# Gated linear attention with a feed-forward network: blocks of two chunks of two batches, and a gather in two steps

## The chip, the cores and the metric

The kernel runs on one core of a Trainium2 chip. The metric is the device time of one execution in microseconds, the median of several runs.

## The reference

Four batches (B), eight heads (H), 768 tokens (S), 48 values in a head (D). A state of 48 by 48 per batch and head is scaled row by row with alpha, gets the outer product of k and v added, and is read with q. The outputs of the heads, side by side, are rows of 384 for 3072 tokens; they go through a feed-forward network (FFN) of 2048 hidden values with a leaky ReLU. The two weights come as 64-bit floats.

```python
for t in range(S):
    state = alpha[:, :, t, :, None] * state + np.einsum('bhd,bhe->bhde', k[:, :, t], v[:, :, t])
    y[:, :, t] = np.einsum('bhd,bhde->bhe', q[:, :, t], state)
...
h = x @ w_in
g = np.maximum(0.01 * h, h)
return (g @ w_out).astype(np.float32)
```

## The kernel before, in words

**Units and blocks.** The attention works on *units*: one chunk of 128 tokens of one batch, with all eight heads. There are 6 chunks and 4 batches, so 24 units, u0 to u23. Four units are a *block* of 512 tokens, and the FFN works on blocks, 0 to 5. Before, a block is one chunk of all four batches, so that the unit which needs a batch's state comes four units behind the one that made it.

**A unit's steps**, in the order of `attention`: `scans` (alpha transposed, its running products pc and rc, on DVE), `scores` (k times q on PE, L348; its wait for the finished ks is what the profile calls L339), `mask_scores` (the triangle: either an ACT copy, L358, and a select on POOL, L359, or one multiplication on DVE, L356; `on_pe` units take two copies and selects, the others one of each kind), `k_tokens` (L371), the next unit's `scaled_q` and `scaled_k`, and `outputs`: the state times q (L388) and the masked scores times v (L394) give y, k times v gives the state's addition kv (L405), then y is split into a high part xh (ACT, L411) and a rest xl (DVE, L412). `next_state` adds to the state (L424 on ACT for the first chunk, L426 on DVE) and POOL scales it (L364). Units u0 to u7, u10 and u11 are transposed on PE (L272), the others on DVE (L281).

**x and the gather.** x lies in the tile `large`, whose 128 partitions are 2 x (48 + 16) rows. Three slots hold six heads in 48 of each 64 rows; heads 6 and 7 are written to a fourth, shared staging slot, and once the four units of a block are there, `gather` moves their rows by two DMAs on SP's queue (L435, 192 KB each) into the 16 free rows of the other three slots. There are seven slots: three for even blocks, three for odd, one staging slot for both. A block's first xh writes the staging slot, so it comes behind the gather of the block before.

**The FFN.** For each of 16 slices of the hidden values, `ffn_in` makes nine matmuls of 512 columns (L479, into `ph`: high and low parts of x and weight), ACT and DVE make the leaky ReLU (L482, L485) and split it into gh and gl (L487, L490), and `ffn_out` makes nine matmuls (L509). Blocks 0 to 4 are written transposed: DVE transposes the result (L526), and SP stores it in pieces of 32 columns of one batch (L531, 16 KB; 16 stores for one of three groups, 48 for a block). Block 5 is written straight.

**The order of the work.** First the attention of blocks 0 and 1 runs, with the first two weight slices converted from 64 bits beside it and the first `ph` groups of block 0 (`STARTS`). Then the FFN of blocks 0 and 1 runs together while the other slices are converted. From block 2 on a block's FFN runs alone, with the steps of later units strewn in by a count (`SL`, `LEAD`, `HELD`). `behind(key)` orders an instruction after another one in the scheduling and adds no semaphore. A scheduler with its own timeline then sets each engine's order; each engine works through its instructions in that order, and SP issues nearly all DMAs in its own.

## Time and profile before

| | |
|---|---|
| runs shown | 566.86, 567.15 and 569.07 us |
| median | 567.15 us |
| the profiled execution | 569.6 us |
| its span in the trace | 567.9 us |
| instructions | 9071 |
| DMA engines, mean share | 39.5% (hardware queue) |

The span runs from the first to the last instruction of the trace. PE is TensorE, PEld its weight loads, DVE VectorE, ACT ScalarE, POOL GpSimd, SP SyncE; SPq is SP's queue. A row of a timeline gives the start and the length in us, the engine, the line, the operation, the tile written and the tiles read, the size, and xN for N instructions alike in a row; in brackets stands how long the engine was idle before it and what ended that. A row of windows gives the stretch, its length, the busy time of PE, PEld, DVE, ACT and POOL, the granted TensorE clock (1.00 is full speed), the DMA share and GB/s. A matmul of plain f32 counts as two in the trace (x8 in the program is x16 there). In the 40 slices a digit is the busy share in tenths, a slice is 14.2 us.

### The profile page before, as it was taken

The numbers are of one execution on the slowest core, as the hardware profiler recorded it, in microseconds if no ns is written. First come the engines' busy times: TensorE is split into PE (matmuls) and PEld (weight loads), VectorE is DVE, ScalarE is ACT, GpSimd is POOL, SyncE is SP. The second block draws the span as 40 slices with busy tenths as digits, with TensorE's granted clock in tenths as the row PEclk, the third lists the DMA queues.
The fourth block names the chain that finished last, engine by engine and source line by source line (L and its number), as shares of the span: only waits on it lengthen the run. The fifth ranks groups of instructions, "written<-read, shape, count | busy, mean of one in ns | idle before, by whom it ended". The sixth has DMA issues, their size and how long they took to land.

```text
span 567.9 us, 9071 instructions
## 1 busy us (share of the span) xinstructions
PE 525.9 (93%) x3262; PEld 439.5 (77%) x3262; DVE 382.9 (67%) x644; ACT 217.5 (38%) x409; POOL 65.0 (11%) x140
## 2 busy tenths in 40 slices
PE   8986869999999999289899999999999999999995
PEld 7765658888887778178788888888888888888994
DVE  6886669889889869519987788577766343343331
ACT  2654534445453334223334334324332432232321
POOL 4444400000000013210211100100100000000000
PEclk9996879999999999659999999999999999999998
DMA  9999333244374122775644633441312101011001
GB/s 148 179 180 194 110 83 99 70 110 113 91 177 72 37 34 44 138 169 108 140 87 102 113 92 58 84 98 27 68 23 34 15 1 29 1 29 28 1 0 61
DMA packets 125795, 46.09 MB, mean 81 GB/s; under 512 B 94960, under 2 KB 123120, under 8 KB 125744
## 3 DMA queue, kind: packets, MB, share of 16 engines
q1 hardware_dynamic: 125744, 45.45, 39.5%
q8 instruction: 27, 0.44, 0.4%
q14 instruction: 24, 0.20, 0.1%
HBM read 38.34 MB, written 4.72 MB: 76 GB/s over the span
## 4 chain that ended last, share of the span: by engine, by line
PE 81%; DVE 8%; DMA 4%; SPq 2%; issue 2%; ACT 1%; POOL 0%; DVEq 0%; ACTq 0%; POOLq 0%
PE ph L479 33%; PE a L509 25%; PE b L509 7%; PE b L394 4%; PE b L348 3%; PE b L388 3%; DMA large<-large 2%; PE b L272 1%; PE ph L165 1%; SPq L531 1%; DVE ks L281 1%; DVE rc L312 1%; PE b L405 1%; DMA small<-in_q_dram 1%; DVE pc L306 1%
## 5 line engine op out<-in xcount | busy, mean ns | idle before, releaser
L479 PE MATMUL ph<-large,w 128*128 128x512 f32 x864 | 219.8, 399 | 8.8 <-DMA large<-large 4.3
L479 PEld LDWEIGHTS ph<-large,w 128*128 128x128 f32 x864 | 162.7, 191 | 44.8 <-issue 5.2
L509 PE MATMUL a<-gh,w 128*128 128x512 f32 x384 | 130.3, 393 | 0.0
L485 DVE TENSOR_TENSOR t<-ph,t 128x512 f32<-128x512 f32 x96 | 65.4, 681 | 93.6 <-ACT t L482 93.5
L482 ACT ACTIVATE t<-ph 128x512 f32<-128x512 f32 x96 | 57.3, 597 | 143.0 <-PE ph L479 140.5
L487 ACT CAST gh<-t 128x512 fp32r<-128x512 f32 x96 | 59.6, 621 | 119.9 <-DVE t L485 117.1
L490 DVE TENSOR_TENSOR gl<-t,gh 128x512 fp32r<-128x512 f32 x96 | 65.8, 685 | 28.0 <-ACT gh L487 19.4
L509 PEld LDWEIGHTS a<-gh,w 128*128 128x128 f32 x384 | 72.0, 188 | 16.0 <-issue 0.6
L509 PE MATMUL a<-gl,w 128*128 128x512 f32 x192 | 75.0, 390 | 0.0
L348 PE MATMUL b<-qs,ks 48*128 48x128 f32 x320 | 31.8, 292 | 12.8 <-DVE ks L339 12.5
L509 PEld LDWEIGHTS a<-gl,w 128*128 128x128 f32 x192 | 36.1, 188 | 7.1
L348 PEld LDWEIGHTS b<-qs,ks 48*128 48x128 f32 x320 | 27.0, 194 | 18.2 <-issue 16.0
L359 POOL TENSOR_SCALAR_AFFINE_SELECT sm<-sm 128x512 f32<-128x512 f32 x34 | 26.0, 775 | 105.5 <-ACT sm L358 105.5
L509 PE MATMUL b<-gh,w 128*128 128x512 f32 x96 | 33.7, 404 | 0.0
L364 POOL TENSOR_TENSOR small<-us,pe 48x192 f32<-48x192 f32 x40 | 22.4, 559 | 76.0 <-DVE us L426 67.0
L316 POOL COPY pe<-pc 128x4 f32<-128x4 f32 x24 | 6.3, 261 | 207.3 <-DVE pc L306 207.1
L394 PE MATMUL b<-sm,small 128*48 128x128 f32 (+1 forms) x368 | 28.6, 279 | 0.2
L388 PE MATMUL b<-qs,small 112*112 112x128 f32 x152 | 21.9, 291 | 6.2 <-DVE large L412 5.8
L388 PEld LDWEIGHTS b<-qs,small 112*112 112x112 f32 x152 | 20.2, 190 | 8.4 <-issue 6.2
L358 ACT COPY sm<-b 128x512 f32<-128x512 f32 x26 | 15.2, 587 | 26.5 <-PE b L348 26.4
L509 PE MATMUL a<-w,gh 128*128 128x384 f32 x96 | 24.3, 338 | 0.0
L394 PEld LDWEIGHTS b<-sm,small 128*48 128x48 f32 (+1 forms) x368 | 20.9, 125 | 4.2 <-POOL sm L359 1.4
(96 smaller groups left out, 622.4 us busy)
## 6 DMA issues: line engine op xcount, KB each, us to landing
raw<-in_moe_w_out_dram SPq DMA_DIRECT2D x16, 384.0 KB, 3.5
small<-in_v_dram SPq DMA_DIRECT2D x24, 192.0 KB, 3.8
raw<-in_moe_w_in_dram SPq DMA_DIRECT2D x32, 144.0 KB, 4.0
out_dram<-o SPq DMA_DIRECT2D x240, 16.0 KB, 1.5
small<-in_alpha_dram SPq DMA_DIRECT2D x30, 96.0 KB, 2.3
small<-in_q_dram SPq DMA_DIRECT2D x28, 96.0 KB, 2.3
small<-in_k_dram SPq DMA_DIRECT2D x28, 96.0 KB, 2.4
large<-large SPq DMA_DIRECT2D x12, 192.0 KB, 4.7
```

Of the source, the lines that this page charges most:

```text
L348: nc.tensor.matmul(ss[s][:, p, :], ks[lo:lo + D, p, :], qs[lo:lo + D, p, :], start=True, stop=True)
L358: made["sm", u] = nc.scalar.copy(sm[s], ss[s])
L359: nc.gpsimd.affine_select(out=sm[s], in_=sm[s], compare_op=ALU.is_ge, fill=0.0, base=0, pattern=[[0, NP], [1, C]], channel_multiplier=-1)
L364: nc.gpsimd.tensor_tensor(*scalings.pop(0))
L388: nc.tensor.matmul(y[0:BR, (p + turn) % NP, :], W[0:BR, p, :], qs[0:BR, p, :], start=p == 0, stop=False, skip_group_check=True)
L394: nc.tensor.matmul(y[lo:lo + m, (p + turn) % NP, :], V[:, c:c + m], masked[u][s][:, p, :], start=not tb and p == 0, stop=p == NP - 1, skip ...
L479: nc.tensor.matmul(ph, w_in_of(f, wn, g), xt[:, g, :], start=n == 0, stop=n == 3 * NG - 1)
L482: put(ordered, "ACT", lambda: nc.scalar.mul(t, ph, 0.01))
L485: put(ordered, "DVE", lambda: nc.vector.tensor_tensor(t, ph, t, ALU.max))
L487: put(ordered, "ACT", lambda: nc.scalar.copy(gh, t))
L490: made["gl", i, f] = put(ordered, "DVE", lambda: nc.vector.tensor_tensor(gl, t, gh.bitcast(F32), ALU.subtract))
L509: nc.tensor.matmul(po, *((w[:, js], gt) if turned else (gt[:, js], w)), start=f == 0 and n == 0, stop=f == NF - 1 and n == 2,)
```

## The change

1. The units are put in another order: a block is now two chunks of two batches, u0 to u3 = (chunk 0, batch 0), (0, 1), (1, 0), (1, 1). `place` gives a unit's columns within x, so that a batch's two chunks stand side by side. A batch's state is now needed two units after it was made (or six). The first chunks' units are u0, u1, u4, u5, the last chunks' u18, u19, u22, u23.
2. x has eight slots: each parity of block has its own staging slot, and the `turn` of the heads is gone.
3. The gather goes in two steps: behind a block's third unit the columns 0 to 384 (four DMAs of 72 KB), behind the fourth the columns 384 to 512 (four of 24 KB). Block 2's are issued on ScalarE's queue, the others on SP's.
4. `mask_scores`: the second half goes to DVE for all units from u6 on; before, u6, u7, u10 and u11 had two ACT copies and two POOL selects.
5. The first output group of block 0 is ordered behind the last y of u7, and some later steps behind other keys ("w", "in", "gl").
6. The transposed output: a store now takes two chunks of one batch (32 KB), so there are 8 stores for a group and 24 for a block.

```diff
-    UPB = B
+    UPB = 4
-    units = [(t, b) for t in range(NC) for b in range(B)]
+    units = [(t0 + t, b0 + b) for t0 in range(0, NC, 2) for b0 in range(0, B, 2) for t in (0, 1) for b in (0, 1)]
...
+    def place(u):
+
+        tb, b = units[u]
+        j = b % 2 * 2 + tb % 2
+        return slice(j * C, (j + 1) * C)
...
-    x_sb, = pieces("large", F32R, (2 * NG + 1, 2, TB))
+    x_sb, = pieces("large", F32R, (2 * (NG + 1), 2, TB))
...
-            if s and not on_pe(u):
+            if s and u >= AHEAD - 2:
...
-        at = i % 2 * NG
-
-        turn = i % 2
+        at = i % 2 * (NG + 1)
...
-        xh, xl = (x_sb[0:BR, at:at + NP, n, j * C:(j + 1) * C] for n in (0, 1))
+        xh, xl = (x_sb[0:BR, at:at + NP, n, place(u)] for n in (0, 1))
...
-    def gather(i):
-
-        at, last = i % 2 * (NG + 1), NG
+    def gather(i, *cols):
+
+        at = i % 2 * (NG + 1)
         xs[i] = [x_sb[:, at:at + NG, n, :] for n in (0, 1)]
-        x = x_sb.bitcast(F32)
-        for lo in (0, HB):
-            made["g", i] = nc.sync.dma_start(
-                x[lo + D:lo + HB, at:at + NG].rearrange("r g n t -> r g (n t)"), x[lo:lo + D, last].rearrange("r n t -> r (n t)")
-            )
+        x = x_sb.bitcast(F32)[:, :, :, slice(*cols)]
+        queue = nc.scalar if i == 2 else nc.sync
+        for n in (0, 1):
+            for lo in (0, HB):
+                made["g", i] = queue.dma_start(x[lo + D:lo + HB, at:at + NG, n], x[lo:lo + D, at + NG, n])
...
-                if u % UPB == UPB - 1:
-                    gather(u // UPB)
+                if u % UPB == UPB - 2:
+                    gather(u // UPB, 0, TB - C)
+                elif u % UPB == UPB - 1:
+                    gather(u // UPB, TB - C, TB)
...
-                for b in range(B):
-                    r = b * S + i * C
+                for n, u in enumerate((i * UPB, i * UPB + 1)):
+                    tb, b = units[u]
+                    r = b * S + tb * C
...
-                        out[r:r + C, c:c + 32].rearrange("(m r) c -> r m c", r=32),
-                        t[32 * a:32 * (a + 1)].rearrange("r (b m c) -> r b m c", b=B, c=32)[:, b],
+                        out[r:r + 2 * C, c:c + 32].rearrange("(m r) c -> r m c", r=32),
+                        t[32 * a:32 * (a + 1)].rearrange("r (b m c) -> r b m c", b=2, c=32)[:, n],
...
-    put_out()
+    with behind("y", AHEAD - 1):
+        put_out()
...
-            with behind("gl", 0, f + FORE):
+            with behind("w", f + FORE + 1) if f + FORE + 1 < NF else behind("gl", 0, f + FORE):
...
-                    with (behind("gl", i, f - 1) if f else behind("x", (i + 1) * UPB - 1)) if held else nullcontext():
+                    with ExitStack() as holds:
+                        if held:
+                            holds.enter_context(behind("in", i, f))
+                            holds.enter_context(behind("gl", i, max(f - 1, 0)))
```

How instructions move shows in the engines' orders. PE at the end of block 1's attention, before: L388 and L394 are u7's y, L405 its kv, `ph` the first matmuls of a slice of block 0, L509 the first output group.

```order
153 L371 MATMUL b<-small,ks 128x112 x4
154 L388 MATMUL a<-qs,small 112x128 x4
155 L479 MATMUL ph<-large,w_786 128x512 x2
156 L394 MATMUL a<-sm,small 48x128
157 L405 MATMUL b<-small,ktok 48x48 x8
158 L509 MATMUL b<-gh,w_571 128x512
159 L509 MATMUL b<-gl,w_571 128x512
160 L509 MATMUL b<-gh,w_571 128x512 x2
161 L509 MATMUL b<-gl,w_571 128x512
162 L509 MATMUL b<-gh,w_571 128x512
163 L394 MATMUL a<-sm,small 48x128 x7
164 L509 MATMUL b<-gh,w_571 128x512
```

The same place after (eight lines further down in the code: L394 and L400 are y, L411 kv, L517 the output group):

```order
152 L379 MATMUL b<-small,ks 128x112 x4
153 L394 MATMUL a<-qs,small 112x128 x4
154 L487 MATMUL ph<-large,w_791 128x512 x2
155 L411 MATMUL b<-small,ktok 48x48 x8
156 L400 MATMUL a<-sm,small 48x128 x8
157 L517 MATMUL b<-gh,w_585 128x512
158 L517 MATMUL b<-gl,w_585 128x512
159 L517 MATMUL b<-gh,w_585 128x512 x2
160 L517 MATMUL b<-gl,w_585 128x512
```

The output group, which stood between y's first matmul and the other seven, now stands behind all eight, and kv ahead of them.

SP between the stores of blocks 0 and 1 and the gather of block 2, before: L531 are stores, L140 and L152 the loads of later units, L435 the gather.

```order
97 L133 DMA small<-in_alpha_dram 128x8x48
98 L531 DMA out_dram<-o 32x4x32 x32
99 L152 DMA small<-in_v_dram 128x8x48
100 L531 DMA out_dram<-o 32x4x32 x16
101 L140 DMA small<-in_alpha_dram 32x4x192 x2
102 L140 DMA small<-in_alpha_dram 32x4x160 x2
103 L140 DMA small<-in_q_dram 32x4x192 x2
104 L140 DMA small<-in_q_dram 32x4x160 x2
105 L140 DMA small<-in_k_dram 32x4x192 x2
106 L140 DMA small<-in_k_dram 32x4x160 x2
107 L152 DMA small<-in_v_dram 128x8x48
108 L435 DMA large<-large 16x3x1024 x2
```

After, L540 are the stores; no gather stands here, since block 2's is on ACT:

```order
103 L141 DMA small<-in_alpha_dram 128x8x48
104 L540 DMA out_dram<-o 32x8x32 x24
105 L160 DMA small<-in_v_dram 128x8x48
106 L148 DMA small<-in_alpha_dram 32x4x192 x2
107 L148 DMA small<-in_alpha_dram 32x4x160 x2
108 L148 DMA small<-in_q_dram 32x4x192 x2
109 L148 DMA small<-in_q_dram 32x4x160 x2
```

Between the same two loads stand 24 stores instead of 48.

PE at the start of block 2's FFN, before: L348 are the scores of u12, behind which stand its other matmuls and then the first three groups of block 2.

```order
455 L348 MATMUL b<-qs,ks 128x128 x8
456 L371 MATMUL b<-small,ks 128x112 x4
457 L388 MATMUL b<-qs,small 112x128 x4
458 L394 MATMUL b<-sm,small 48x128
459 L405 MATMUL b<-small,ktok 48x48 x8
460 L479 MATMUL ph<-large,w_571 128x512 x9
461 L479 MATMUL ph<-large,w_786 128x512 x9
462 L479 MATMUL ph<-large,w_897 128x512 x9
```

After, rows 445 to 449 are u11's matmuls, and block 2's groups follow at once (a group's first matmul stands apart in two of them):

```order
445 L356 MATMUL b<-qs,ks 128x128 x8
446 L379 MATMUL b<-small,ks 128x112 x4
447 L394 MATMUL b<-qs,small 112x128 x4
448 L400 MATMUL b<-sm,small 48x128 x8
449 L411 MATMUL b<-small,ktok 48x48 x8
450 L487 MATMUL ph<-large,w_585 128x512
451 L487 MATMUL ph<-large,w_791 128x512
452 L487 MATMUL ph<-large,w_585 128x512 x8
453 L487 MATMUL ph<-large,w_791 128x512 x8
454 L487 MATMUL ph<-large,w_907 128x512 x9
```

u12's scores come 25 rows further down, among block 2's output groups.

More of the change, by code (lines that the diff above doesn't have):

```diff
@@ L377, in outputs @@
         tb, b = units[u]
-        i, j = divmod(u, UPB)
+        i = u // UPB
         pe, qs, ktok = live[u][:3]
         V, W = vals_sb[u % NV], state[b]
-        at = i % 2 * NG
-        turn = i % 2
+        at = i % 2 * (NG + 1)
         y = banks4()
@@ L388, in outputs @@
                 nc.tensor.matmul(
-                    y[0:BR, (p + turn) % NP, :], W[0:BR, p, :], qs[0:BR, p, :], start=p == 0, stop=False, skip_group_check=True
+                    y[0:BR, p, :], W[0:BR, p, :], qs[0:BR, p, :], start=p == 0, stop=False, skip_group_check=True
                 )
@@ L393, in outputs @@
                 c = (2 * p + s) * D
-                nc.tensor.matmul(
-                    y[lo:lo + m, (p + turn) % NP, :], V[:, c:c + m], masked[u][s][:, p, :],
+                made["y", u] = nc.tensor.matmul(
+                    y[lo:lo + m, p, :], V[:, c:c + m], masked[u][s][:, p, :],
                     start=not tb and p == 0, stop=p == NP - 1, skip_group_check=True,
@@ L478, in ffn_in @@
             for wn, xt in ((HIGH, xh), (HIGH, xl), (LOW, xh)):
-                nc.tensor.matmul(ph, w_in_of(f, wn, g), xt[:, g, :], start=n == 0, stop=n == 3 * NG - 1)
+                made["in", i, f] = nc.tensor.matmul(ph, w_in_of(f, wn, g), xt[:, g, :], start=n == 0, stop=n == 3 * NG - 1)
                 n += 1
@@ L505, in ffn_out @@
         for j, po in enumerate(pos[i]):
-            js = slice(j * P, (j + 1) * P)
+            js = slice(j * P, (j + 1) * P) if turned else place(i * UPB + j)
             for n, (gt, wn) in enumerate(((gh, HIGH), (gl, HIGH), (gh, LOW)) if turned else ((gh, HIGH), (gh, LOW), (gl, HIGH))):
```

## The prediction

> **What bounds the kernel now.** I read the page first: its busy times and its slices show which engine is short and where it isn't full.
>
> ```profile
> span 567.9 us, 9071 instructions
> PE 525.9 (93%) x3262; PEld 439.5 (77%) x3262; DVE 382.9 (67%) x644; ACT 217.5 (38%) x409; POOL 65.0 (11%) x140
> ...
> PE   8986869999999999289899999999999999999995
> ...
> PEclk9996879999999999659999999999999999999998
> ```
>
> PE is busy for 93% of the span, and its matmuls are the same before and after the change. So a gain can only come from the slices in which PE waits or has a low clock. A slice is 14.2 us: the weak ones are the first six (0 to 85 us) and those at 227 to 256 us. I then read PE's timeline there, which names the end of each wait. First place, near 47 us (columns: start, us, engine, line, operation, count, and in brackets the idle time before it):
>
> ```profile
> 47.48 2.02 PE L388 MATMUL b<-qs,small 112*112 112x128 f32 x8 [5.81 <-DVE large L412]
> 49.29 1.06 PE L272 MATMUL b<-small 128*128 128x128 f32 x4
> 52.34 0.73 PE L479 MATMUL ph<-large,w 128*128 128x512 f32 x2
> ...
> 56.60 0.60 PE L272 MATMUL b<-small 128*128 128x128 f32 x4
> 57.03 1.04 PE L388 MATMUL b<-qs,small 112*112 112x128 f32 x8
> ```
>
> ```profile
> 46.02 0.58 ACT L411 CAST large<-b 112x512 fp32r<-112x512 f32 x1 [6.29 <-DMA large<-large]
> ```
>
> ```profile
> 39.88 6.04 DMA large<-large
> 71.92 4.68 DMA large<-large
> ```
>
> The last two rows are from the chain: both gathers lie on it. At 46.02 ACT copies the first xh of block 1 and has waited 6.29 us for block 0's gather, because both blocks stage heads 6 and 7 in one slot. PE waits behind it for 5.81 us and then runs at a low clock: the same eight matmuls take 2.02 us here and 1.04 at 57.03, the same four transposes 1.06 and 0.60.
>
> Second place, 62 to 82 us, the last unit of block 1 (u7):
>
> ```profile
> 62.30 3.28 POOL L359 TENSOR_SCALAR_AFFINE_SELECT sm<-sm 128x512 f32<-128x512 f32 x2 [0.68 <-ACT sm L358]
> ```
>
> ```profile
> 65.05 0.39 PE L394 MATMUL a<-sm,small 128*48 128x128 f32 x1 [2.62 <-POOL sm L359]
> ...
> 66.22 0.80 PE L509 MATMUL b<-gh,w 128*128 128x512 f32 x1
> ...
> 68.86 1.07 PE L394 MATMUL a<-sm,small 128*48 128x128 f32 x14
> ...
> 76.74 5.03 PE L479 MATMUL ph<-large,w 128*128 128x512 f32 x11 [4.27 <-DMA large<-large]
> ```
>
> PE waits 2.62 us for u7's masks. It has begun y when six matmuls of the first output group cut in at 66.22 (2.64 us to 68.86), then y ends, xh, xl and the gather follow, and PE waits 4.27 us for the gather at 76.74, again with a low clock behind it.
>
> Third place, 230 to 257 us, from the last unit of block 2 (u11) to block 2's FFN:
>
> ```profile
> 225.41 1.71 PE L348 MATMUL b<-qs,ks 48*128 48x128 f32 x16 [0.23 <-DVE ks L339]
> ...
> 229.07 0.99 PE L394 MATMUL b<-sm,small 128*48 128x128 f32 x13
> 242.34 2.08 PE L348 MATMUL b<-qs,ks 48*128 48x128 f32 x16 [12.28 <-DVE ks L339]
> ...
> 249.29 8.09 PE L479 MATMUL ph<-large,w 128*128 128x512 f32 x27 [0.89 <-PE b L405]
> ```
>
> ```profile
> 231.06 0.72 DVE L526 STREAM_TRANSPOSE o<-a 128x512 f32<-128x512 f32 x1 [4.33 <-DMA out_dram<-o]
> ```
>
> ```profile
> 204.04 16.42 SPq L531 DMA_DIRECT2D out_dram<-o  x32
> ...
> 221.05 8.70 SPq L531 DMA_DIRECT2D out_dram<-o  x16
> 229.84 1.81 SPq L140 DMA_DIRECT2D small<-in_alpha_dram  x4
> ...
> 236.03 1.23 SPq L435 DMA_DIRECT2D large<-large  x2
> ```
>
> SP issues 48 stores for 16.42 + 8.70 = 25.1 us. Behind them stand the loads of u12 (229.84) and the gather (236.03). DVE's output transpose at 231.06 has waited 4.33 us for stores to free its buffer, and u11's xl stands behind it. PE meets u12's scores first in its order, so the gathered block waits behind a unit whose loads are late: 12.28 us.
>
> **The change part by part.** The durations are those of the profiled execution: 569.6 us, of which 567.9 are the span and 1.7 lie around it. It is 2.45 above the median of 567.15, so 2.45 comes off at the end.
>
> ```profile
> 173.72 3.79 PE L479 MATMUL ph<-large,w 128*128 128x512 f32 x16
> ```
>
> ```profile
> out_dram<-o SPq DMA_DIRECT2D x240, 16.0 KB, 1.5
> ...
> large<-large SPq DMA_DIRECT2D x12, 192.0 KB, 4.7
> ```
>
> From these: a warm 512-column matmul takes 3.79 / 16, about 0.23 us; a gather of 192 KB lands 4.7 us after its issue, a store of 16 KB 1.5; a gather takes SP 1.23 / 2 = 0.61 us to issue, a store 25.1 / 48 = 0.52. The new gather pieces (72 and 24 KB) have no row: a landing between 1.5 and 4.7 us.
>
> *First place.* With slots apart, xh no longer waits: 5.81 goes, and of the low clock (2.02 - 1.04) + (1.06 - 0.60) = 1.4; together 7.2. What is late next: block 0's first two ph matmuls (52.34) would be reached at 52.34 - 7.2 = 45.1. The four issues of the gather's second step take 4 x 0.61 = 2.4 from 39.23 on, to 41.7, if the first step has gone ahead behind u2; the last piece lands 1.5 to 6.04 later, at 43.2 to 47.7. I take 47.2, near the row of this very place, since the queue is full there. So 2.1 is given back (0 to 2.6). Net **5.1** (4.6 to 7.2).
>
> ```profile
> L356 DVE TENSOR_TENSOR sm<-b,small 128x512 f32<-128x512 f32 x14 | 9.5, 678 | 3.2 <-PE b L348 3.2
> ...
> 71.31 1.21 SPq L435 DMA_DIRECT2D large<-large  x2
> ```
>
> ```profile
> 32.00:72.00 40.00, 30.02 (x296) 25.07 (x293) 28.22 (x51) 18.39 (x40) 16.55 (x22) 0.83 0.76 158
> 66.00:68.00 2.00, 2.00 (x11) 1.62 (x8) 1.59 (x3) 0.00 (x0) 1.15 (x2) 0.50 0.93 305
> ```
>
> *Second place.* u6 and u7 give one of two masks to DVE: POOL is spared 3.28 / 2 = 1.64 ahead of y, DVE gets 2 x 0.68 = 1.4. I count 0.2. DVE must be able to come earlier at all: in 32 to 72 it is busy 28.2 of 40 us (third of the busy times; the clock stands behind the five), so after the masks u7's xl can come at most 40 - 28.2 - 1.4 = 10.4 us earlier; places 1 and 2 up to there want less than that. From y's start to block 1's ph it is 76.74 - 65.05 = 11.7 us. Now y runs in one piece (0.23 + 1.07 = 1.3), then xh 0.58 and xl 0.69, three issues ahead of the last one (1.8), a landing of 2.4, which I set nearer to the store's 1.5 since the queue is light by then: 6.8. The output group, moved behind y, and seven ph matmuls of block 0 (16 x 0.23 = 3.6) fill most of it, and PE still waits about 1.9. The saving is 4.9. The low clock behind it costs 5.03 - 11 x 0.23 = 2.5; I keep 2.0 of this, since after the wait of 2.62 us the clock in 66 to 68 was 0.50 too: 0.5 saved. Net **5.6** (2 to 9: nothing of the landing gained, or all waits gone).
>
> The Trainium skill (TensorE: Matmul & The Clock Gate, Part 1: The HAM clock gate) says that the clock is halved after an idle window of some 3.4 us and comes back after as much work. By it a wait of 1.9 us costs no clock, place 2 would gain 2.0 more and the sum would come to 544.7; the row of 66 to 68, behind a wait of only 2.62 us, differs, and the sum goes by the row.
>
> *Third place.* PE goes from 230.06 to 257.38, 27.3 us, through work that is worth 229.07 - 225.41 = 3.7 (u11's same steps, for u12) and 27 x 0.23 = 6.2: 17.4 are lost. Now 24 stores stand on SP instead of 48 (24 x 0.52 = 12.5 us), the gather goes through ACT's queue past them, and block 2's ph stands ahead of u12's scores. What is left is y to ph: xh 0.58, xl 0.69, issues 1.8, landing 2.4, less the kv matmuls that now stand behind y:
>
> ```profile
> 280.36 0.53 PE L405 MATMUL b<-small,ktok 128*48 128x48 f32 x16
> ```
>
> So 5.5 - 0.5 = 5.0, and a low clock of 2.0 to 2.5 as at both places before (8.09 - 6.2, 5.03 - 2.5): 2.3. DVE's two masks more per two units add up to 0.4. The saving is 17.4 - 5.0 - 2.3 - 0.4 = **9.7** (5 to 15: the gather on ACT waits for stores, or PE waits for nothing).
>
> *At no cost.* ACT issues eight DMAs (4.9 us); ACT is busy 38%. A store of 32 KB instead of 16: 0.52 if issue doesn't grow; an alpha load, 1024 runs, took less:
>
> ```profile
> 171.23 0.37 SPq L133 DMA_DIRECT2D small<-in_alpha_dram  x1
> ```
>
> If it does grow, that is a rival below. The gathers of blocks 3 to 5 are issued while PE has the block before to do. State updates now follow after two units instead of four; POOL, which scales the state, is busy 11%. u12's work on DVE, some 8 us, moves into block 2's FFN:
>
> ```profile
> 256.00:264.00 8.00, 8.00 (x46) 6.34 (x45) 8.00 (x15) 2.92 (x5) 0.37 (x2) 1.00 0.38 72
> ```
>
> ```profile
> 282.48 2.37 PE L479 MATMUL ph<-large,w 128*128 128x512 f32 x9 [1.59 <-DVE t L485]
> ```
>
> DVE is full there, and one wait of 1.59 us shows; I count nothing and allow 2 either way.
>
> Sum: 5.1 + 5.6 + 9.7 = 20.4. 569.6 - 20.4 = 549.2, less 2.45: **546.7 us**.
>
> **The rivals.** *Small gathers land late.* The first step's four issues don't get out of the way (4 x 0.61 = 2.4 at each of three places) and a 24-KB piece lands as late as 192 KB (4.7 instead of 2.4 at two places, 0.5 more at the first): 7.2 + 4.6 + 0.5 = 12.3, so **559.0**. For it: eight gathers in place of two at every block. Against it: the store row, 16 KB in 1.5 us. The Trainium skill (DMA: Bandwidth & Descriptors, Rules for kernel authors) asks to coalesce small transfers and says that those under 64 KB are mostly overhead; that rule speaks against this split, and the store row does not bear it out for the landing.
>
> *ACT's queue isn't free.* The DMAs of both queues share eight counters in turn, and each waits for the one eight before. Then the gather on ACT waits for stores all the same; place 3 falls to its lower end, 4.7 less: **551.4**.
>
> *Larger stores cost more to issue.* With 1.04 us each, SP is as long as before, and DVE's output transpose waits in front of new work twice (2 x 4.33 = 8.7): **555.4**. Against it stands the alpha load.
>
> *DVE becomes the bound in block 2 (slower).* The 1.59-us wait comes in each of the 16 slices: 25.4, so **572.1**. It decides from 13 such waits on (20.4 / 1.59). For it: DVE 8.00 of 8.00. Against it: one such wait now, and only 8 us of work come.
>
> *More is gained.* All of place 2's waits and clock (2.62 + 4.27 + 2.5 = 9.4) and 15 at place 3, 7.2 at the first: 31.6, **535.5**. *It doesn't do what it says*: block 0's ph waits as xh did, and loads keep u12 in front: within 2.8 us of before.
>
> **How the numbers follow.** Forecast 0.65, small gathers 0.10, ACT's queue 0.10, larger stores 0.05, DVE's bound 0.05, more gained 0.04, no change 0.01. A measurement of this kernel tells about 0.5% (2.8 us) from no change. Faster: 0.65 + 0.10 + 0.10 + 0.05 + 0.04 = 0.94; same 0.01; slower 0.05. The range of **538 to 556** takes in the forecast with most of its bounds, ACT's queue and larger stores, and leaves out some 0.2.
>
> **What would show it.** In the profile after: no wait of ACT for a gather near 40 us, but a wait of PE of about 2 for block 0's ph; y of u7 in one piece and a wait near 2 before block 1's ph; near 225 us, a wait of 4 to 5 for a gather instead of 12.28 for ks; 24 stores in 12 us. Wrong it is if gather pieces take over 4 us to land, if PE waits for DVE's t in most slices of block 2, or if new waits stand at the places of units 16 to 23, where I see none.

## The result, and the profile after

| | before | after |
|---|---|---|
| median | 568.11 us (566.86 to 571.2, 4 runs) | 553.54 us (552.67 to 553.84, 4 runs) |
| profiled execution | 569.6 us | 553.5 us |
| its span | 567.9 us | 551.5 us |

The ratio is 0.973 (95% interval 0.969 to 0.978): the changed kernel is faster by 2.7%, or 14.6 us of the medians. The forecast was 546.7 with a range of 538 to 556. In 23 later runs, beside b_held and b_four, the kernel before has a median of 567.32, so that its profiled execution, at 569.6, lay 2.3 above; that of the changed kernel lies on its median.

The page of the changed kernel, the same rows as before:

```profile
span 551.5 us, 8989 instructions
...
PE 525.3 (95%) x3262; PEld 436.4 (79%) x3262; DVE 383.9 (70%) x648; ACT 215.2 (39%) x405; POOL 64.3 (12%) x136
...
PE   8989799999999997799999999999999999999994
...
PEclk9999899999999999699999999999999999999998
```

PE's busy time is the same but for 0.6 us; the span is shorter by what PE waited. The weak slices at the start are fewer, and of the weak stretch in the middle two slices are left (207 to 234 us).

**First place.** ACT's copy of block 1's first xh, block 0's gather on SP's queue, and PE from the first ph of block 0 on:

```profile
40.03 0.59 ACT L417 CAST large<-b 112x512 fp32r<-112x512 f32 x1 [0.21 <-PE b L400]
```

```profile
34.74 1.39 SPq L443 DMA_DIRECT2D large<-large  x2
...
36.82 2.12 SPq L443 DMA_DIRECT2D large<-large  x3
...
39.66 2.67 SPq L443 DMA_DIRECT2D large<-large  x3
```

```profile
45.92 0.74 PE L487 MATMUL ph<-large,w 128*128 128x512 f32 x2
...
58.38 0.56 PE L411 MATMUL b<-small,ktok 128*48 128x48 f32 x16 [0.98 <-ACT ktok L381]
60.30 1.95 PE L400 MATMUL a<-sm,small 128*48 128x128 f32 x16 [1.36 <-POOL sm L367]
65.04 2.33 PE L487 MATMUL ph<-large,w 128*128 128x512 f32 x8
67.84 4.14 PE L487 MATMUL ph<-large,w 128*128 128x512 f32 x17 [0.47 <-DVE pw L262]
```

The copy has waited 0.21 us instead of 6.29. The gather's eight DMAs leave from 34.74 on, the last at 41.75, and that one has landed at 43.7. Block 0's first ph starts at 45.92 instead of 52.34, and nothing stands in brackets: it doesn't wait for the gather.

**Second place.** It follows in the last fence: u7's y runs in one piece at 60.30, after 1.36 us for POOL's select, and the matmuls at 65.04 are seven of block 0 and the first of block 1, which doesn't wait for the gather in this execution. The clock behind the short waits is low all the same (the value behind the five busy times):

```profile
56.00:60.00 4.00, 1.63 (x22) 0.87 (x20) 4.00 (x7) 3.56 (x8) 1.97 (x1) 1.00 0.97 247
60.00:62.00 2.00, 1.70 (x16) 1.51 (x16) 1.47 (x3) 0.00 (x0) 1.83 (x3) 0.56 0.59 129
62.00:64.00 2.00, 2.00 (x9) 1.49 (x6) 1.08 (x2) 0.59 (x1) 0.00 (x0) 0.58 0.66 203
```

PE was busy for 1.63 of 4 us there, with three waits of which none is longer than 1.36, and the clock fell to 0.56. It doesn't do so in every execution. e_held, a kernel of the next section, has the same program up to here:

```profile
60.07 1.08 PE L400 MATMUL a<-sm,small 128*48 128x128 f32 x16 [1.35 <-POOL sm L367]
...
67.15 0.47 PE L487 MATMUL ph<-large,w 128*128 128x512 f32 x1 [2.14 <-DMA large<-large]
67.90 5.71 PE L487 MATMUL ph<-large,w 128*128 128x512 f32 x17 [0.28 <-DMA large<-large]
```

Behind the same waits its clock stayed at 1.00 (rows of 2 us from 56 to 68). y took 1.08 us instead of 1.95, so PE came sooner to block 1's ph, waited 2.14 us there for the gather, and ran at 0.56 from 68 to 70. With the same program up to here e_late waits 2.77 us at this point, e_sp 1.50, e_pool 0.62, and e_store2 does not wait. So the 4.27 us for the gather have become 0 to 2.8, and where the wait is missing, a low clock before it has taken the time. Behind 2.14 and 2.77 us (e_held, e_late) the clock fell to 0.56 and 0.50, behind 1.50 (e_sp) it stayed at 1.00. The Trainium skill (TensorE: Matmul & The Clock Gate, Part 1: The HAM clock gate) has the clock halved after an idle window of some 3.4 us; each wait in these rows is shorter, so these traces differ from it, as the row of 66 to 68 of the kernel before did.

**Third place.** PE, then ACT and its queue (ACTq), then SP's queue:

```profile
215.00 1.04 PE L394 MATMUL b<-qs,small 112*112 112x128 f32 x8
219.57 1.08 PE L400 MATMUL b<-sm,small 128*48 128x128 f32 x16 [3.54 <-POOL sm L367]
...
224.92 9.48 PE L487 MATMUL ph<-large,w 128*128 128x512 f32 x27 [3.61 <-DMA large<-large]
```

```profile
212.67 0.59 ACT L417 CAST large<-b 112x512 fp32r<-112x512 f32 x1 [2.00 <-PE b L400]
217.39 0.67 ACTq L443 DMA_DIRECT2D large<-large  x1
218.16 0.59 ACT L366 COPY sm<-b 128x512 f32<-128x512 f32 x1 [4.91 <-DMA out_dram<-o]
...
222.21 2.58 ACTq L443 DMA_DIRECT2D large<-large  x4
```

```profile
191.62 13.19 SPq L540 DMA_DIRECT2D out_dram<-o  x24
...
214.87 1.02 SPq L540 DMA_DIRECT2D out_dram<-o  x2
215.98 1.83 SPq L148 DMA_DIRECT2D small<-in_q_dram  x4
```

The 12.28 us for u12's ks are gone. In their place stands a wait that the change brought: u10's xh is there at 213.3, but ACT issues the first DMA of the gather only at 217.39, and u11's mask copy, queued behind it on ACT, has waited 4.91 us, as the row says for a store. PE then waits 3.54 for that mask and 3.61 for the gather. The order of ACT, with the counters that each instruction waits for, shows how they are tied:

```
166 L443 DMA large<-large 16x3x384 [waits DMAHW4_49,Activation_49]
167 L366 COPY sm<-b 128x512 [waits PE_49,Pool_49]
168 L443 DMA large<-large 16x3x384 [waits DMAHW6_49,DVE_49]
```

DMAHW0 to DMAHW7 are eight counters that the DMAs of SP's and ACT's queues use in turn. A DMA takes a counter over only when the DMA that had it before has landed. In the program's order DMAHW4 was held by the first of the two stores that SP issued at 214.87.

**By stretches.** To see where the time went I counted the FFN matmuls in PE's trace (those that write ph from x, and those that read gh or gl, 1776 in each trace) and took the start of the 60th (behind places 1 and 2), the 576th (the last of blocks 0 and 1, ahead of place 3), the 864th (the last of block 2, behind it) and the 1756th. At each of these points every kernel has the same number of attention matmuls behind it. The kernels below the first two rows are those of the next section; each row is one execution.

| kernel | to 60 | 60 to 576 | 576 to 864 | 864 to 1756 |
|---|---|---|---|---|
| before | 86.7 | 122.8 | 126.9 | 220.8 |
| after | 75.0 | 121.8 | 122.5 | 220.8 |
| e_share | 74.7 | 121.8 | 122.9 | 220.8 |
| e_one | 77.2 | 121.8 | 128.8 | 220.8 |
| e_order | 80.4 | 121.8 | 122.5 | 220.8 |
| e_outmask | 75.3 | 121.7 | 120.5 | 220.8 |
| e_store2 | 75.2 | 121.8 | 121.9 | 220.8 |
| e_held | 76.6 | 121.8 | 123.7 | 220.8 |
| e_sp | 74.3 | 121.8 | 122.6 | 220.8 |
| e_late | 77.2 | 121.8 | 122.8 | 220.8 |
| e_pool | 75.4 | 121.7 | 119.8 | 220.8 |
| e_pair | 76.4 | 121.1 | 125.2 | 220.8 |
| b_held | 85.7 | 122.8 | 124.1 | 220.8 |
| b_four | 85.3 | 122.8 | 123.7 | 220.8 |

Kernels with the same program up to the 60th matmul (after, e_store2, e_held, e_sp, e_late, e_pool) lie between 74.3 and 77.2 there, with the waits and clocks of the second place told above, so this stretch of one execution is good to about 3 us. What is closer than that is read from the medians.

### The profile page after: what moved, and what is told of

It is laid out like the page before. It is cut to its first block, busy times and chain, and to the rows that moved or that the text cites. A ratio compares the mean times of both kernels' runs of the same rounds, so it can differ in the third digit from the quotient of the medians.

```text
span 551.5 us, 8989 instructions
## 1 busy us (share of the span) xinstructions
PE 525.3 (95%) x3262; PEld 436.4 (79%) x3262; DVE 383.9 (70%) x648; ACT 215.2 (39%) x405; POOL 64.3 (12%) x136
## 4 chain that ended last, share of the span: by engine, by line
PE 76%; DVE 11%; DMA 5%; SPq 3%; issue 2%; POOL 1%; ACT 1%; DVEq 0%
PE ph L487 31%; PE a L517 26%; PE b L517 6%; PE b L400 3%; PE b L356 3%; PE b L394 2%; DMA small<-in_alpha_dram 2%; DMA raw<-in_moe_w_out_dram 2%; SPq L540 1%; DVE rc L320 1%; DMA small<-in_k_dram 1%; DVE pc L314 1%; PE b L280 1%; DVE e L289 1%; DVE ks L289 1%
## 5 line engine op out<-in xcount | busy, mean ns | idle before, releaser
L517 PE MATMUL a<-gh,w 128*128 128x512 f32 x384 | 130.7, 394 | 0.0
L517 PEld LDWEIGHTS a<-gh,w 128*128 128x128 f32 x384 | 71.9, 188 | 16.2 <-issue 0.7
L517 PE MATMUL a<-gl,w 128*128 128x512 f32 x192 | 75.2, 392 | 0.0
L517 PEld LDWEIGHTS a<-gl,w 128*128 128x128 f32 x192 | 36.1, 188 | 7.1
L356 PE MATMUL b<-qs,ks 48*128 48x128 f32 x320 | 34.6, 284 | 0.3 <-DVE ks L347 0.2
L400 PE MATMUL b<-sm,small 128*48 128x128 f32 (+1 forms) x368 | 28.4, 277 | 6.7 <-POOL sm L367 6.1
L356 PEld LDWEIGHTS b<-qs,ks 48*128 48x128 f32 x320 | 29.1, 187 | 6.5 <-issue 4.4
L367 POOL TENSOR_SCALAR_AFFINE_SELECT sm<-sm 128x512 f32<-128x512 f32 x30 | 22.6, 764 | 93.2 <-ACT sm L366 92.6
L517 PE MATMUL b<-gh,w 128*128 128x512 f32 x96 | 33.0, 398 | 0.0
L324 POOL COPY pe<-pc 128x4 f32<-128x4 f32 x24 | 7.6, 316 | 206.0 <-DVE pc L314 206.0
L400 PEld LDWEIGHTS b<-sm,small 128*48 128x48 f32 (+1 forms) x368 | 20.6, 124 | 11.0 <-POOL sm L367 7.5
L517 PE MATMUL a<-w,gh 128*128 128x384 f32 x96 | 24.4, 338 | 0.0
L517 PEld LDWEIGHTS b<-gh,w 128*128 128x128 f32 x96 | 18.3, 192 | 4.6 <-ACT gh L495 0.6
L366 ACT COPY sm<-b 128x512 f32<-128x512 f32 x23 | 13.5, 587 | 17.8 <-PE b L356 12.9
L394 PEld LDWEIGHTS b<-qs,small 112*112 112x112 f32 x152 | 18.7, 176 | 2.2 <-DVE large L418 0.9
```

The costliest lines, as they stand in the source:

```text
L356: nc.tensor.matmul(ss[s][:, p, :], ks[lo:lo + D, p, :], qs[lo:lo + D, p, :], start=True, stop=True)
L366: made["sm", u] = nc.scalar.copy(sm[s], ss[s])
L367: nc.gpsimd.affine_select(out=sm[s], in_=sm[s], compare_op=ALU.is_ge, fill=0.0, base=0, pattern=[[0, NP], [1, C]], channel_multiplier=-1)
L394: nc.tensor.matmul(y[0:BR, p, :], W[0:BR, p, :], qs[0:BR, p, :], start=p == 0, stop=False, skip_group_check=True)
L400: made["y", u] = nc.tensor.matmul(y[lo:lo + m, p, :], V[:, c:c + m], masked[u][s][:, p, :], start=not tb and p == 0, stop=p == NP - 1, ski ...
L517: nc.tensor.matmul(po, *((w[:, js], gt) if turned else (gt[:, js], w)), start=f == 0 and n == 0, stop=f == NF - 1 and n == 2,)
```

## The experiments

All were timed in five rounds beside the kernel before, whose medians were 567.78, 567.82 and 567.32 in the three groups. The after kernel's 553.54 (552.67 to 553.84) is the value to compare with for those named e_. It was measured apart from them.

**e_share: one staging slot again.**

```diff
-    x_sb, = pieces("large", F32R, (2 * (NG + 1), 2, TB))
+    x_sb, = pieces("large", F32R, (2 * NG + 1, 2, TB))
...
-        at = i % 2 * (NG + 1)
+        at = i % 2 * NG
+
+        turn = i % 2
...
-                    y[0:BR, p, :], W[0:BR, p, :], qs[0:BR, p, :], start=p == 0, stop=False, skip_group_check=True
+                    y[0:BR, (p + turn) % NP, :], W[0:BR, p, :], qs[0:BR, p, :], start=p == 0, stop=False, skip_group_check=True
...
-                made["g", i] = queue.dma_start(x[lo + D:lo + HB, at:at + NG, n], x[lo:lo + D, at + NG, n])
+                made["g", i] = queue.dma_start(x[lo + D:lo + HB, at:at + NG, n], x[lo:lo + D, NG, n])
```

> One staging slot for both parities of block again, the rest as changed. Theory A: block 1's first xh waits for block 0's gather again, as before the change: the 6.4 us that the trace shows gained by block 0's first ph are lost, 559 to 561. Rival B: the gather's first step takes the columns that block 1's first unit writes out of the slot early, so that the split alone frees it: 553 to 555.5.

553.55 us (552.18 to 554.45; ratio 0.975, 0.972 to 0.977). Theory A falls. The first step's four DMAs leave from 33.47 to 37.3, and block 1's first xh, which writes the columns that this step has taken away, doesn't wait:

```profile
33.47 0.58 SPq L445 DMA_DIRECT2D large<-large  x1
34.73 0.64 SPq L445 DMA_DIRECT2D large<-large  x1
36.05 1.23 SPq L445 DMA_DIRECT2D large<-large  x2
...
39.46 2.58 SPq L445 DMA_DIRECT2D large<-large  x3
```

```profile
39.81 0.58 ACT L419 CAST large<-b 112x512 fp32r<-112x512 f32 x1 [0.22 <-PE b L402]
```

**e_one: the gather in one step of four DMAs of 96 KB.**

```diff
-                if u % UPB == UPB - 2:
-                    gather(u // UPB, 0, TB - C)
-                elif u % UPB == UPB - 1:
-                    gather(u // UPB, TB - C, TB)
+                if u % UPB == UPB - 1:
+                    gather(u // UPB, 0, TB)
```

> Each gather in one step of four DMAs of 96 KB behind the last unit. Theory A: the landing gets longer by 1 to 2 us at the three places where PE waits for it (blocks 0 to 2), but u11's mask copy no longer stands behind a gather: -3.5 + 3 to 6, so 553 to 556. Rival B, that small transfers are mostly overhead: half as many DMAs, faster by 2 to 5 us, 548.5 to 551.5.

560.82 us (557.96 to 562.63; ratio 0.986, 0.982 to 0.989): 7.3 slower than after, beyond both theories. The first place stays good (the slots are apart here). The 77.2 us to the 60th matmul lie within the spread of the after kernel's program. At the third place 6.3 us go (128.8 against 122.5): the four issues on ACT take 6.87 us, and PE waits twice for them:

```profile
223.32 6.87 ACTq L443 DMA_DIRECT2D large<-large  x4
```

```profile
228.57 1.19 PE L485 MATMUL ph<-large,w 128*128 128x512 f32 x2 [8.90 <-DMA large<-large]
...
232.52 5.82 PE L485 MATMUL ph<-large,w 128*128 128x512 f32 x18 [2.76 <-DMA large<-large]
```

**e_order: blocks, stores and keys alone.** To e_share's and e_one's edits it adds:

```diff
-        queue = nc.scalar if i == 2 else nc.sync
+        queue = nc.sync
...
-            if s and u >= AHEAD - 2:
+            if s and not on_pe(u):
...
-    with behind("y", AHEAD - 1):
-        put_out()
+    put_out()
```

> Only the blocks of two chunks of two batches, with their stores of 32 KB, and the steps ordered behind other keys: one staging slot, the gather in one step of four DMAs on SP's queue, the old mask rule, the first output group not ordered. Theory A: places 1 and 2 stay as before the change (11.4 us less gained), the third keeps what the fewer stores bring (5 to 7): 561 to 564. Rival B: with the gather on SP behind its stores the third place gains nothing either: 566 to 569.

558.48 us (557.74 to 561.84; ratio 0.985, 0.982 to 0.988): better than either theory, 9.3 less than before. The first place is lost, as it must be with one slot and one step: ACT waits 5.02 us for the gather, and PE as long behind it.

```profile
44.60 0.59 ACT L419 CAST large<-b 112x512 fp32r<-112x512 f32 x1 [5.02 <-DMA large<-large]
```

```profile
47.29 0.69 PE L402 MATMUL b<-sm,small 128*64 128x128 f32 x2 [5.02 <-POOL sm L367]
...
72.44 3.34 PE L487 MATMUL ph<-large,w 128*128 128x512 f32 x11 [0.30 <-DMA large<-large]
```

The second place is as good as in the after kernel: the wait before block 1's ph is 0.30, without the split and without the ordered output group. The third is as good too (122.5 in both), with the gather on SP behind its stores.

**e_outmask: the old mask rule, and the first output group not ordered.**

```diff
-            if s and u >= AHEAD - 2:
+            if s and not on_pe(u):
...
-    with behind("y", AHEAD - 1):
-        put_out()
+    put_out()
```

> The changed kernel with the old mask rule and the first output group not ordered behind u7's y. Theory A, as predicted: the group then stands within y instead of filling the wait for the gather, and POOL makes one select more ahead of y: 555.5 to 558. Rival B: the smaller gather lands so soon that there is nothing left to fill: 553 to 555.

552.25 us (549.64 to 552.82; ratio 0.972, 0.969 to 0.975). Theory A falls: neither part brings anything. The wait before block 1's ph is 0.31 us here. At the third place PE waits 1.54 us for the mask and 4.17 for the gather, 5.71 in all against 3.54 + 3.61 = 7.15 in the after kernel. So the two parts may even cost something, but the runs of the two kernels just overlap, and it isn't shown.

**b_four: the kernel before with each gather as four DMAs.**

```diff
-        for lo in (0, HB):
-            made["g", i] = nc.sync.dma_start(
-                x[lo + D:lo + HB, at:at + NG].rearrange("r g n t -> r g (n t)"), x[lo:lo + D, last].rearrange("r n t -> r (n t)")
-            )
+        for n in (0, 1):
+            for lo in (0, HB):
+                made["g", i] = nc.sync.dma_start(x[lo + D:lo + HB, at:at + NG, n], x[lo:lo + D, last, n])
```

> The kernel before with each gather as four DMAs of 96 KB instead of two of 192, at the same place. Theory A: a DMA lands the sooner the smaller it is (4.7 us for 192 KB, 3.2 for 96 where it was measured), and PE waits for the landing at three places: 1.5 less at each, against two more issues of 0.6: 564 to 567.5. Rival B, small transfers are mostly overhead: 568 to 571.

566.02 us (565.0 to 568.63, 12 runs) beside 567.32; ratio 0.997 (0.995 to 0.999). Theory A holds, at the small end of its gain, by an interval that just leaves out 1: PE's wait for the gather at the second place is 2.11 us instead of 4.27.

```profile
75.70 0.94 PE L478 MATMUL ph<-large,w 128*128 128x512 f32 x3 [2.11 <-DMA large<-large]
```

**b_held: the kernel before with the new keys for the held steps.**

```diff
-                nc.tensor.matmul(ph, w_in_of(f, wn, g), xt[:, g, :], start=n == 0, stop=n == 3 * NG - 1)
+                made["in", i, f] = nc.tensor.matmul(ph, w_in_of(f, wn, g), xt[:, g, :], start=n == 0, stop=n == 3 * NG - 1)
...
-                    with (behind("gl", i, f - 1) if f else behind("x", (i + 1) * UPB - 1)) if held else nullcontext():
+                    with ExitStack() as holds:
+                        if held:
+                            holds.enter_context(behind("in", i, f))
+                            holds.enter_context(behind("gl", i, max(f - 1, 0)))
                         next(st, None)
```

> The kernel before with only the new keys for the held steps, so that block 2's first ph groups stand ahead of u12's scores on PE. Theory A: the third place's gain comes from this order, since PE waited 12.28 us for u12's ks, whose loads stand behind 48 stores, while block 2's x lay gathered; what stays is the wait for the gather, issued at 236: 561 to 564 in place of 567.8. Rival B: the gain comes from the blocks of two chunks (DVE's output transposes, the loads), and this alone gives nothing: 566.5 to 569.

567.52 us (565.67 to 568.6, 12 runs) beside 567.32; ratio 1.000 (0.998 to 1.002). Nothing: PE meets block 2's ph first, but the gather is still issued at 233 behind 48 stores and a part of the loads, and PE waits for that. It would have waited so in the kernel before: there the gather's two DMAs, issued at 236.03 and 236.67, landed at 242.1 and 243.2, while u12's ks was there at 242.34.

```profile
219.90 8.49 SPq L531 DMA_DIRECT2D out_dram<-o  x16
...
233.24 1.23 SPq L435 DMA_DIRECT2D large<-large  x2
```

```profile
238.86 9.28 PE L479 MATMUL ph<-large,w 128*128 128x512 f32 x27 [9.94 <-DMA large<-large]
```

**e_held: the changed kernel with the old keys.**

```diff
-                    with ExitStack() as holds:
-                        if held:
-                            holds.enter_context(behind("in", i, f))
-                            holds.enter_context(behind("gl", i, max(f - 1, 0)))
+                    with (behind("gl", i, f - 1) if f else behind("x", (i + 1) * UPB - 1)) if held else nullcontext():
```

> The changed kernel with the old keys for the held steps; u12's scores then stand behind the second group of block 2 instead of the sixth. Theory A: PE waits there for u12's ks, whose loads are late, and block 2 starts with a wait: 555.5 to 560. Rival B: with 24 stores the loads are there in time, and the keys are worth nothing: 552.5 to 555.

555.14 us (552.04 to 556.81; ratio 0.977, 0.974 to 0.981). It lies between the theories, and the ranges overlap; the keys are worth 0 to 3 us, and which isn't settled.

**e_store2: stores of 16 KB for blocks 0 and 1.** Each store of these blocks is cut into its two chunks.

```diff
-                    nc.sync.dma_start(
-                        out[r:r + 2 * C, c:c + 32].rearrange("(m r) c -> r m c", r=32),
-                        t[32 * a:32 * (a + 1)].rearrange("r (b m c) -> r b m c", b=2, c=32)[:, n],
-                    )
+                    for half in (0, 1) if i < 2 else (None,):
+                        if half is None:
...
+                            continue
+                        nc.sync.dma_start(
+                            out[r + half * C:r + (half + 1) * C, c:c + 32].rearrange("(m r) c -> r m c", r=32),
+                            t[32 * a:32 * (a + 1)].rearrange("r (b m c) -> r b m c", b=4, c=32)[:, 2 * n + half],
+                        )
```

> Stores of 16 KB for blocks 0 and 1, 96 instead of 48; 24 of the 48 more stand ahead of block 2's gather. Theory A: the number of DMAs that SP issues sets the third place; each costs 0.5 us whatever its size, so block 2's FFN starts 6 to 12 us later: 559.5 to 566. Rival B: what counts there is bytes or the landing, and the time stays within 1 us of 553.5.

553.82 us (552.72 to 555.08; ratio 0.976, 0.973 to 0.978). Theory A falls. SP is busy with 48 stores for 23.57 us and reaches the loads of u12 only at 215.98, but PE's waits ahead of block 2 come to 7.2 us (2.92 for an xl of block 2, 4.27 for the gather) as in the after kernel (3.54 + 3.61), because u12 isn't needed before block 2's first groups. So the number of stores is not what sets the third place once u12 stands behind block 2 and the gather is on ACT's queue; with the gather on SP it was not tried.

```profile
191.81 23.57 SPq L547 DMA_DIRECT2D out_dram<-o  x48
...
215.98 3.01 SPq L148 DMA_DIRECT2D small<-in_alpha_dram  x4
```

```profile
225.85 8.13 PE L487 MATMUL ph<-large,w 128*128 128x512 f32 x27 [4.27 <-DMA large<-large]
```

**e_sp, e_late, e_pool: where block 2's gather is issued.** All on SP; on ACT, but the first step behind u11's mask copy; on GpSimd.

```diff
-        queue = nc.scalar if i == 2 else nc.sync
+        queue = nc.sync
```

> Block 2's gather on SP's queue like the others. Theory A: u11's mask copy is free at once (PE's wait of 3.54 us before y goes), but the second step stands behind what SP has to issue and waits longer than 3.61 us on PE: 551 to 556. Rival B, that the queue of its own is what the change gains at this place: the gather waits behind stores and loads as before the change, 558 or more.

```diff
-                if u % UPB == UPB - 2:
+                if u % UPB == UPB - 2 and u // UPB != 2:
...
                 k_tokens(u)
+                if u == 3 * UPB - 1:
+                    with behind("sm", u):
+                        gather(2, 0, TB - C)
```

> Theory A: the first step of block 2's gather on ScalarE's queue waits for a DMA counter that SP's DMAs hold, and u11's mask copy stands behind it; that is the wait of 4.91 us on ACT and 3.54 us on PE before u11's y. With the first step behind u11's copies PE's wait before y falls under 1 us; up to four more issues (2.4 us) then stand behind y, so 549.5 to 552.5 us in place of 553.5. Rival B: u11's masks are late for another reason (POOL, DVE), or the gather's landing sets the start of block 2 anyway: 553.5 +- 1.

```diff
-        queue = nc.scalar if i == 2 else nc.sync
+        queue = nc.gpsimd if i == 2 else nc.sync
```

> Block 2's gather on GpSimd's queue, which has counters of its own. Theory A: at the third place the gather waits for SP's DMAs, through shared counters on ScalarE's queue and through the queue's order on SP's; free of both, u11's mask copy and the gather start as soon as x is there, the waits of 3.54 and 3.61 us on PE fall to 3 or 4 in all, and the time is 548 to 551. Rival B: the DMA engines themselves are full there, or issuing on GpSimd costs as much as it saves: 552.5 to 555.

| | median (range) | ratio | PE's wait for the mask | for the gather |
|---|---|---|---|---|
| after, ACT | 553.54 (552.67 to 553.84) | 0.973 (0.969 to 0.978) | 3.54 | 3.61 |
| e_sp | 554.32 (551.85 to 555.32) | 0.975 (0.972 to 0.978) | none | 8.96 |
| e_late | 554.00 (552.36 to 556.02) | 0.974 (0.971 to 0.978) | none | 7.11, then 1.73 |
| e_pool | 550.72 (549.57 to 552.40) | 0.970 (0.968 to 0.973) | 1.11 | 4.85 |

e_late frees the mask copy and gains nothing: the gather leaves at 222.00 instead of 217.39, again behind a counter that SP's loads hold, and what PE no longer waits for the mask it waits for the gather.

```profile
222.00 1.31 ACTq L443 DMA_DIRECT2D large<-large  x2
223.35 0.59 ACT L417 CAST large<-b 112x512 fp32r<-112x512 f32 x1 [4.13 <-DMA small<-in_k_dram]
```

```profile
226.77 1.19 PE L490 MATMUL ph<-large,w 128*128 128x512 f32 x2 [7.11 <-DMA large<-large]
```

e_sp comes out the same with the gather in SP's own order. On GpSimd, whose DMAs use eight counters of their own in the program (DMASW0 to DMASW7), the first DMA leaves at 213.97, as soon as u10's xh is there, and the sum of PE's two waits is 5.96 instead of 7.15. The pieces don't land sooner on this queue (3.5 us for 72 KB and 2.6 for 24, on ACT's 3.2 and 1.9); they leave sooner. The 27 ph matmuls behind the wait take 8.22 us instead of 9.48, which together with the waits makes 2.45 of the 2.7 us that this stretch gains (119.8 against 122.5):

```profile
213.97 0.69 POOL L443 DMA_DIRECT2D large<-large  x1 [3.30 <-ACT large L417]
215.73 1.58 POOL L443 DMA_DIRECT2D large<-large  x3
220.06 0.57 POOL L443 DMA_DIRECT2D large<-large  x1 [1.01 <-ACT large L417]
```

It is the fastest kernel of the study: all of its runs lie below all of the after kernel's, by 2.8 us in the median; the intervals of the two ratios overlap by a little. e_share, timed beside it and on ACT's queue, is at 553.55.

**e_pair: a unit's scores kept together.** In the after kernel u13, u14 and u15 have their scores in two halves, far apart on PE (x8 in the trace), and a half takes as long as a whole one:

```profile
246.57 1.16 PE L356 MATMUL b<-qs,ks 48*128 48x128 f32 x16
255.48 1.16 PE L356 MATMUL b<-qs,ks 48*128 48x128 f32 x8
261.79 1.16 PE L356 MATMUL b<-qs,ks 48*128 48x128 f32 x8
```

```diff
+        m = None
         for p in range(NP):
             for s, lo in ((0, 0), (1, HB)):
+                with tc.issue_after(m.ins) if m else nullcontext():
-                nc.tensor.matmul(ss[s][:, p, :], ks[lo:lo + D, p, :], qs[lo:lo + D, p, :], start=True, stop=True)
+                    m = nc.tensor.matmul(ss[s][:, p, :], ks[lo:lo + D, p, :], qs[lo:lo + D, p, :], start=True, stop=True)
```

> Theory A: the scores of u13, u14 and u15 now stand in two halves of four matmuls on PE, which then don't run two at a time; each half takes 1.1 us, as the whole did before, so three units lose 3 x 1.1 = 3.3 us. With each matmul of a unit ordered behind the one before (one alone, then seven together) 550 to 551.5 us. Rival B: DVE is full in block 2's first slices and sets their pace, so PE's saving is waited away: 553.5 +- 1.

555.76 us (554.79 to 558.0; ratio 0.978, 0.974 to 0.981): slower by 2.2. Inconclusive on the halves, since the edit moved the third place too: three gather DMAs now stand ahead of u11's mask copy on ACT, which waits 8.04 us, and PE waits 6.87 behind it. The order within a unit does count: u10's and u11's scores, which take 1.71 us each in the after kernel with one half's four behind the other's, take 1.16 here, where the halves alternate.

## Why the prediction was right, and where its steps were wrong

The sign and the range held; the point was 6.8 too low. On the profiled execution 16.1 us were gained (569.6 to 553.5) where the sum said 20.4. By the stretches, which add up to the 16.4 us of the span: 11.7 up to the 60th matmul (foreseen 5.1 + 5.6 = 10.7), 1.0 to the 576th, 4.4 at the third place (foreseen 9.7), nothing from there to the 1756th, and 0.7 lost behind it. The range held because two of the three places were sized well.

**First place: the size holds, the reason was half of it.** The wait and its low clock went, 6.4 us at block 0's first ph; the 2.1 that I let the gather give back didn't come: its last DMA left at 41.75, as foreseen (41.7), but landed 2.0 us later, where I took 5.5. But "With slots apart, xh no longer waits" names a part that isn't needed: e_share has one slot and loses nothing. e_one has slots apart and no split, and keeps the place too. Each of the two suffices, and only e_order, without both, has the wait back.

**Second place: the size holds (11.7 - 6.4 = 5.3 against 5.6), the reasons only in part.** I had the output group fill the landing and the masks shift to DVE. Undoing both costs nothing (e_outmask), and e_order, with neither and without the split, passes from the third to the 31st FFN matmul in 17.9 us against 18.4 in the after kernel and 23.3 before. Four DMAs instead of two give some 1.3 to 2 of that (b_four: 1.3 in the median over all places, 2.1 of PE's wait). The rest comes with the block order, and by what wait isn't settled. The wait of 1.9 that I kept for the gather is not in the profile of after, but it is in those of e_sp, e_held and e_late (1.50 to 2.77). Behind the two longer ones the next 17 matmuls take 5.71 and 5.73 us instead of 4.12, so the 2.0 kept for the low clock was of the right size as well. In the profile of after the low clock comes ahead of that point and takes the wait's place.

**Third place: the term that was mis-sized, and the step that failed is "the gather goes through ACT's queue past them".** It doesn't get past them, and 4.4 us were gained there instead of 9.7. The queues share eight counters, as the second rival said (chance 0.10, price 4.7). That rival's mechanism is what the trace shows, with u11's mask copy stuck behind the waiting issue, which I hadn't priced. PE's waits come to 7.15 us where the sum kept 5.0, and the low clock behind them to 9.48 - 6.2 = 3.3 where it kept 2.3. Freed from the counters, e_pool gains 2.8. The queue of its own is worth nothing (e_sp). "Now 24 stores stand on SP instead of 48", too, was counted as a cause and isn't one in the after kernel (e_store2), and the keys that put block 2's ph ahead of u12 give nothing alone (b_held). "So the gathered block waits behind a unit whose loads are late" misread the 12.28 us: the gather itself landed only at 243.2. What works is only shown as a whole: e_order, with block order, stores and keys together, is 9.3 us under the kernel before, of which the finer gather explains 1.3. Undone singly in the changed kernel, the stores cost nothing (e_store2) and the keys 0 to 3 us (e_held). The block order was undone in no run, so what it gives by itself stays open. So does the size at this place: b_held and b_four pass the stretch in 124.1 and 123.7 us against 126.9, with medians at most 1.3 below that of the kernel before, so that some of the 4.4 may be the excess of the one profiled execution.

**A cost that I didn't see.** The prediction took PE's matmuls to be "the same before and after the change" and so put their time at nothing. Their number is the same. But the halved scores of u13 to u15 cost about 1.1 us each on PE by the rows above, with PE busy and no wait in the profile; these 3.3 us lie in the stretch of the third place. e_pair did not show that they can be had back.

**The offset.** 2.45 was taken off because the profiled execution lay above the median. The excess is not in the after kernel's profile: its 553.5 equals its median. That it sat in waits which the change removes is likely, by the third place of b_held and b_four, and not shown. If it did, then taken off behind the sum it was counted twice: 569.6 - 20.4 would have been 549.2. Of the 6.8 by which the point missed, 4.3 is the sum (20.4 - 16.1) and 2.45 this.

The other rivals: gather pieces did not land late (1.9 us for 24 KB, 2.7 for 72), larger stores did not cost more to issue (13.19 / 24 = 0.55 against 0.52), and DVE did not become the bound, since one wait of PE for `t` is left, of 0.3 us.

## What to carry to other kernels

Here a queue on another engine freed a DMA only where it shared nothing with the full one (e_pool, not after or e_late): read from the order which counters its instructions wait for, and what stands behind it on its engine, which waits too. A wait that two edits remove is removed by either, so undo them one at a time and both together before saying which one worked. A wait that is missing in one profile may be there in the next execution of the same program, with a low clock in its place: read a second trace before calling it gone. Set the offset of a profiled execution against its median before the sum, not behind it, when the excess may lie in the waits that the change takes away.

## What the runs showed of the hardware

On SP's queue a DMA within the on-chip memory lands the later the larger it is, without a step between 24 and 192 KB. The rows of after and of e_order (median us to landing at the end):

```profile
large<-large SPq DMA_DIRECT2D x20, 72.0 KB, 2.7
...
large<-large SPq DMA_DIRECT2D x20, 24.0 KB, 1.9
```

```profile
large<-large SPq DMA_DIRECT2D x24, 96.0 KB, 3.2
```

With the 4.7 us for 192 KB of the kernel before these lie on 1.5 us and 0.017 us for a KB. Cutting a gather on which PE waits from 192 to 96 KB gained 1.3 us by the medians (b_four). The Trainium skill (DMA: Bandwidth & Descriptors, Rules for kernel authors) asks to coalesce small transfers and calls those under 64 KB mostly overhead. The line agrees for 24 KB, where 1.5 of 1.9 us are its fixed part; b_four's pieces are above 64 KB and don't test the rule. And eight score matmuls of 48 rows (x16 in the trace), in both halves of the array, take 1.16 us together, as long as four of one half alone.
